# Strassen's seven products for the expert layers that run outside attention, with partial sums carried from PSUM bank to PSUM bank

## The chip, the core and the metric

One core of one Trainium2 chip. The metric is the device time of one execution in microseconds. Before the change it is 869.21 us, the median of three runs (868.94 to 869.37). The profile shows one execution of its own, with a span of 865.8 us from the first to the last instruction.

## The reference

Three layers follow each other on 3072 tokens (4 batches of 768) with 256 features (8 heads of 32): a chunked scan, a mixture of four experts, and a gated dense layer, all in float32.

```python
# scan ("attention" below), per batch and head, chunk by chunk
M = einsum(Cc, Bc) * L            # L = exp(cum_i - cum_j), causal
y = M @ xc + (Cc @ state) * exp(cum)
...
def _moe_ref(x, domain_probs, w1, w2):          # 4 experts, 256 -> 1024 -> 256
    p = domain_probs / (domain_probs.sum(-1, keepdims=True) + 1e-09)
    for e in range(E):
        h = np.maximum(x @ w1[e], 0.0)          # the "first layer" of expert e
        out += p[:, e:e + 1] * (h @ w2[e])      # its "second layer"
...
def _moe2_ref(x, w_gate, w_val, w_out):         # 256 -> 1536 -> 256, weights in float64
    g = x @ w_gate
    return (g / (1 + exp(-g)) * (x @ w_val)) @ w_out
```

## The kernel before

Every number is kept as a high part and a low part (tiles named `..h` and `..l`, the low part being the remainder), so one product of a 128x128 weight block with 512 tokens takes three matmuls: high by high, low by high, high by low. Tokens lie along the free dimension. `xh` and `xl` hold the tokens, `acc` the sum over the experts, six blocks of 512 tokens each.

All instructions stand in the order in which the code writes them; each engine works through its own list. Side work (attention steps, weight preparation, loads) is put between the matmuls by a table `todo`: a *unit* is one hidden chunk of 128 columns of one expert on one token tile, it has two half-slots, and `add` or `spread` puts functions into them.

- **Experts 0 and 1, inside attention** (`units1`): 7 token tiles (two of 256 tokens, five of 512), 2 experts, 8 hidden chunks. `m_hidden` runs the 6 matmuls of the first layer into a PSUM bank, ScalarE writes `hh` with a Relu, VectorE writes `hl` with the remainder; three units later `m_out` runs the 6 matmuls of the second layer into two output banks. The attention steps of chunk q (`points(q)`) lie around slot 66+8(q-8).
- **Experts 2 and 3, after attention** (`units23`): the same for 6 blocks of 512 tokens. Meanwhile the float64 weights of the dense layer are loaded and turned into high and low parts (`dense_chunk`: nine VectorE steps for a half, sums by GpSimd, splits by ScalarE and GpSimd) and stored to DRAM.
- **Dense layer**: for pairs of token blocks and *quads* of 2x128 hidden columns, `dense_hidden` already uses Strassen's scheme: 7 products in place of 8. With the 2x2 blocks of weights A and tokens B and the shared sums S1..S4 and T1..T4, each product goes to one of four banks X, Y, Z, W, and shared sums are added by VectorE from SBUF temporaries c1, u, v.

PSUM has eight banks: `h0..h2` for hidden sums, `po0, po1` for outputs and, once attention is done, `d0..d2`.

Of the kernel before, what the change touches and what calls it, by code (L numbers as in the profile page):

```python
# [7 lines left out]
F32 = mybir.dt.float32  # L8
F32R = mybir.dt.float32r
# [3 lines left out]
AX = mybir.AxisListType  # L13


@with_exitstack
def kernel(ctx: ExitStack, tc: tile.TileContext, nat_d, bc_d, bc0_d, a_d, probs, w1, w2, wg, wv, wo, out):
# [32 lines left out]
    sizes = [256] * 2 + [512] * 5  # L50
    offs = [sum(sizes[:i]) for i in range(len(sizes))]
    NTILE = len(sizes)
    assert sum(sizes) == NT
    BN = 512
    NBLK = NT // BN
    NPAIR = NBLK // 2
    NQD = FC2 // 2
    W7 = 7 * P
# [3 lines left out]
    hpool = ctx.enter_context(tc.tile_pool(name="hpool", bufs=LAG + 1))  # L62
# [10 lines left out]
    xh, xl, acc = ([v[o // BN][:, :, o % BN:o % BN + n] for o, n in zip(offs, sizes)] for v in (bxh, bxl, bacc))  # L73
    probs_d = dram.tile([E, NT], F32, name="probs_d")
# [395 lines left out]
    def a_done(q, keep=False):  # L470
        r = Q[q] if keep else Q.pop(q)
        y = r["y"]
        t, o = tile_of(q)
        yv = y[:, :KD * P].rearrange("p (k i) -> p k i", k=KD)
# [56 lines left out]
    def hidden_bank(n):  # L531
        turn[0] += 1
        return bank(*banks[turn[0] % min(len(banks), 4)])[:, :n]

    def place(u):

        e, t, f = u
        if e < 2:
            return offs[t], sizes[t], xh[t], xl[t], acc[t]
        return t * BN, BN, bxh[t], bxl[t], bacc[t]  # L540
# [15 lines left out]
    def m_out(u, later=None):  # L556
        e, t, f = u
        _, n, _, _, sm = place(u)
        if f == 0:
            opsum[e, t] = out_banks(n, len(banks) > 3 and t % 2 == 0)  # L560
# [9 lines left out]
        if later is None:  # L570
            tmp = [mpool.tile([P, 512], F32, tag="mb", name="tmp")[:, :n] for _ in range(KD)]
        else:
            both = raw_p.tile([P, KD, 512], F32, tag="raw", name="tmp")
            tmp = [both[:, d, :n] for d in range(KD)]
        for d in range(KD):
            nc.vector.tensor_tensor(out=tmp[d], in0=po[d], in1=pb, op=ALU.mult)

        def adds(engine=nc.vector):
            for d in range(KD):
                engine.tensor_tensor(out=sm[:, d, :], in0=sm[:, d, :], in1=tmp[d], op=ALU.add)  # L580

        later.append(adds) if later is not None else adds()

# [11 lines left out]
    def dense_src(c):  # L595
        g, what = divmod(c, 3)
        if what == 2:
            return wo[g * FG:(g + 1) * FG, :].rearrange("(k p) d -> p k d", p=P), NG, DM
        w = wg if what == 0 else wv
        return w[:, g * FG:(g + 1) * FG].rearrange("(k p) f -> p k f", p=P), KD, FG  # L600

    def dense_chunk(c, resident):
# [4 lines left out]
        src, k, n = dense_src(c)  # L607
        g, what = divmod(c, 3)
        kz = k // 2
        r = {}  # L610

        def load(z):
            def fn():
                r[z] = raw_p.tile([P, kz, n, 2], I32, tag="raw", name="f64")
                nc.sync.dma_start(
                    out=r[z].rearrange("p k n w -> p k (n w)"), in_=src[:, z * kz:(z + 1) * kz, :].bitcast(I32)
                )
            return fn

        def step(z, i):  # L620
            def fn():
                if (z, i) == (0, 0):
                    r["w"] = dpools["cv"].tile([P, 2, 4 * P], I32, tag="wr", name="dr", bufs=2)
                words = r[z].rearrange("p k n w -> p (k n) w")
                if what == 2:
                    m = r["w"][:, z, :]
                    lo, hi = words[:, :, 0], words[:, :, 1]
                else:
                    m = r["w"][:, :, z * 2 * P:(z + 1) * 2 * P]
                    lo, hi = (words[:, :, x].rearrange("p (j n) -> p j n", j=2) for x in range(2))  # L630
                if i == 0:
                    V.tensor_scalar(out=m, in0=hi, scalar1=20, scalar2=0x7FF, op0=ALU.logical_shift_right, op1=ALU.bitwise_and)
                elif i == 1:
                    V.tensor_scalar(out=m, in0=m, scalar1=896.0, scalar2=0.0, op0=ALU.subtract, op1=ALU.max)
                elif i == 2:
                    V.tensor_scalar(out=m, in0=m, scalar1=255.0, scalar2=8388608.0, op0=ALU.min, op1=ALU.mult)
                elif i == 3:
                    V.scalar_tensor_tensor(out=m, in0=hi, scalar=-0x80000000, in1=m, op0=ALU.bitwise_and, op1=ALU.bitwise_or)
                elif i == 4:
                    V.tensor_scalar(out=hi, in0=hi, scalar1=0xFFFFF, scalar2=3, op0=ALU.bitwise_and, op1=ALU.logical_shift_left)  # L640
                elif i == 5:
                    V.tensor_tensor(out=m, in0=m, in1=hi, op=ALU.bitwise_or)
                elif i == 6:
                    V.tensor_scalar(out=lo, in0=lo, scalar1=28, scalar2=None, op0=ALU.logical_shift_right)
                else:
# [429 lines left out]
```

## Time and profile before

| what | us |
|---|---|
| median of three runs | 869.21 |
| this profiled execution, span | 865.8 |
| TensorE (PE) busy | 855.1, 99% of the span |
| VectorE (DVE) busy | 578.7, 67% |
| ScalarE (ACT) busy | 343.7, 40% |
| GpSimd (POOL) busy | 333.0, 38% |

The span leaves out 3.4 us of the median. A matmul of 128x512 is listed with 0.39 us, but the next one starts 0.23 us later: matmuls overlap, so their starts are what to count, and a busy share of 100% does not by itself say that no start was late.

### The profile page before, as it was taken

The numbers are of one execution on the slowest core, as the hardware profiler recorded it, in microseconds if no ns is written. First come the engines' busy times: TensorE is split into PE (matmuls) and PEld (weight loads), VectorE is DVE, ScalarE is ACT, GpSimd is POOL, SyncE is SP. The second block draws the span as 40 slices with busy tenths as digits, with TensorE's granted clock in tenths as the row PEclk, the third lists the DMA queues.
The fourth block names the chain that finished last, engine by engine and source line by source line (L and its number), as shares of the span: only waits on it lengthen the run. The fifth ranks groups of instructions, "written<-read, shape, count | busy, mean of one in ns | idle before, by whom it ended". The sixth has DMA issues, their size and how long they took to land.

```text
span 865.8 us, 12236 instructions
## 1 busy us (share of the span) xinstructions
PE 855.1 (99%) x4490; PEld 708.8 (82%) x4490; DVE 578.7 (67%) x881; ACT 343.7 (40%) x605; POOL 333.0 (38%) x282
## 2 busy tenths in 40 slices
PE   8999999999999999999999999999999999999998
PEld 7898888888888888888888888887888878888886
DVE  6987556656554446767768587766676767667665
ACT  6664444444443333322233223324444444434443
POOL 5965323323331021321033126515563664535251
PEclk9999999999999999999999999999999999999999
DMA  7844443343350032144234302535344274437301
GB/s 245 281 155 142 134 135 102 117 137 102 103 170 20 25 110 87 60 146 146 86 99 180 110 25 79 201 122 188 132 156 151 92 265 135 173 109 268 110 1 48
DMA packets 46003, 111.38 MB, mean 129 GB/s; under 512 B 5048, under 2 KB 12920, under 8 KB 45944
## 3 DMA queue, kind: packets, MB, share of 16 engines
q1 hardware_dynamic: 45944, 110.61, 38.0%
q8 instruction: 35, 0.57, 0.3%
q14 instruction: 24, 0.20, 0.1%
HBM read 93.14 MB, written 17.45 MB: 128 GB/s over the span
## 4 chain that ended last, share of the span: by engine, by line
PE 87%; DVE 5%; POOL 3%; ACT 2%; issue 1%; DMA 1%; SPq 0%; POOLq 0%; ACTq 0%; DVEq 0%
PE h L509 24%; PE po L517 21%; PE h L804 14%; PE d L517 6%; PE d L804 5%; PE d L875 5%; PE po L875 5%; PE d L509 3%; PE ypsum L438 1%; PE scores L392 1%; PE ypsum L401 1%; POOL w_l L125 1%; POOL ws L666 1%; DVE hl L553 1%; POOL L L344 1%
## 5 line engine op out<-in xcount | busy, mean ns | idle before, releaser
L553 DVE SCALAR_TENSOR_TENSOR hl<-h,hh 128x512 fp32r<-128x512 f32 (+1 forms) x184 | 117.7, 642 | 163.3 <-ACT hh L552 163.1
L552 ACT ACTIVATE hh<-h 128x512 fp32r<-128x512 f32 (+1 forms) x184 | 102.6, 559 | 280.6 <-PE h L509 272.1
L842 POOL TENSOR_TENSOR al<-s,ah 128x512 fp32r<-128x512 f32 x70 | 103.5, 1505 | 124.1 <-ACT ah L840 114.6
L509 PE MATMUL h<-xh,w_h 128*128 128x512 f32 (+1 forms) x368 | 138.9, 377 | 2.6 <-DVE hl L553 2.1
L509 PE MATMUL h<-xl,w_h 128*128 128x512 f32 (+1 forms) x368 | 137.2, 373 | 0.0
L509 PE MATMUL h<-xh,w_l 128*128 128x512 f32 (+1 forms) x368 | 136.7, 372 | 0.0
L517 PE MATMUL po<-hh,w_h 128*128 128x512 f32 (+1 forms) x320 | 118.4, 370 | 0.6 <-ACT L L350 0.6
L517 PE MATMUL po<-hh,w_l 128*128 128x512 f32 (+1 forms) x320 | 118.0, 369 | 0.0
L517 PE MATMUL po<-hl,w_h 128*128 128x512 f32 (+1 forms) x320 | 117.8, 368 | 0.0
L840 ACT ACTIVATE ah<-s 128x512 fp32r<-128x512 f32 x72 | 45.3, 632 | 100.3 <-DVE s L837 84.7
L509 PEld LDWEIGHTS h<-xh,w_h 128*128 128x128 f32 x368 | 69.3, 188 | 18.1 <-issue 3.6
L509 PEld LDWEIGHTS h<-xl,w_h 128*128 128x128 f32 x368 | 69.3, 188 | 14.0 <-DVE xl L477 2.1
L509 PEld LDWEIGHTS h<-xh,w_l 128*128 128x128 f32 x368 | 69.3, 188 | 11.3
L517 PEld LDWEIGHTS po<-hh,w_h 128*128 128x128 f32 x320 | 60.2, 188 | 11.4 <-issue 1.1
L517 PEld LDWEIGHTS po<-hl,w_h 128*128 128x128 f32 x320 | 60.3, 188 | 10.1
L517 PEld LDWEIGHTS po<-hh,w_l 128*128 128x128 f32 x320 | 60.3, 188 | 9.7
L359 POOL TENSOR_TENSOR Bs<-bc,Bs 64x512 fp32r<-64x512 f32 x22 | 32.4, 1475 | 82.9 <-issue 71.3
L821 DVE TENSOR_TENSOR u<-h,c 128x512 f32<-128x512 f32 x36 | 24.9, 690 | 56.8 <-PE h L804 37.3
L832 ACT ACTIVATE s<-s 128x512 f32<-128x512 f32 x54 | 33.4, 629 | 43.3 <-DVE s L831 42.5
L804 PE MATMUL h<-xh,wq_h 128*128 128x512 f32 x128 | 50.1, 392 | 0.2 <-ACT s L832 0.2
L804 PE MATMUL h<-xh,wq_l 128*128 128x512 f32 x128 | 49.8, 389 | 0.0
L804 PE MATMUL h<-xl,wq_h 128*128 128x512 f32 x128 | 49.8, 389 | 0.0
(222 smaller groups left out, 1730.2 us busy)
## 6 DMA issues: line engine op xcount, KB each, us to landing
wq_h<-wd_d SPq DMA_DIRECT2D x32, 448.0 KB
wq_l<-wd_d SPq DMA_DIRECT2D x32, 448.0 KB
bc<-in_bc_dram SPq DMA_DIRECT2D x22, 512.0 KB
L<-crow_d SPq DMA_DIRECT2D x22, 512.0 KB
wq_o<-wo_d SPq DMA_DIRECT2D x16, 512.0 KB
nat<-in_nat_dram SPq DMA_DIRECT2D x24, 256.0 KB
raw<-in_w_dram SPq DMA_DIRECT2D x11, 512.0 KB
pbc<-probs_d SPq DMA_DIRECT2D x22, 256.0 KB
```

Of the source, the lines that this page charges most:

```text
L125: engine.tensor_tensor(out=lo[:, part], in0=raw[:, part], in1=hi[:, part].bitcast(F32), op=ALU.subtract)
L359: nc.gpsimd.tensor_tensor(out=r["Bs"][64:], in0=r["Br"][64:], in1=r["Bs"][64:].bitcast(F32), op=ALU.subtract)
L509: nc.tensor.matmul(ps, w[:, k, fs], v[:, k, :], start=(i == 0), stop=(i == len(ops) - 1))
L517: nc.tensor.matmul(po[d], w[:, fc, dsl], x, start=(first and i == 0), stop=(last and i == 2))
L552: nc.scalar.activation(out=hh, in_=ph, func=AF.Relu)
L553: nc.vector.scalar_tensor_tensor(out=hl, in0=ph, scalar=0.0, in1=hh.bitcast(F32), op0=ALU.max, op1=ALU.subtract)
L804: nc.tensor.matmul(ps, x[:, ws], y, start=(start and i == 0), stop=(i == 2), skip_group_check=True)
L821: V.tensor_tensor(out=u, in0=Y, in1=c1, op=ALU.add)
L832: nc.scalar.activation(out=s[key], in_=ps if add is None else s[key], func=AF.Silu)
L840: nc.scalar.activation(out=ah, in_=av, func=AF.Copy)
L842: low.tensor_tensor(out=al, in0=av, in1=ah.bitcast(F32), op=ALU.subtract)
L875: nc.tensor.matmul(po[d][:, zs], x[:, dsl], y[:, zs], start=(first and i == 0), stop=(last and i == 2), skip_group_check=True)
```

## The change

Only five token tiles (2048 tokens) stay inside attention; the attention steps of a chunk now lie 5.8 half-slots apart in place of 8. The last 1024 tokens of experts 0 and 1, and all of experts 2 and 3, move behind attention and run in 8 blocks (expert, pair of token blocks), each of 4 quads of 256 hidden columns (32 quads). A quad takes 7 products in place of 8 for the first layer (21 matmuls for 24) and the same 24 for the second. The shared sums do not pass through SBUF: ScalarE copies a bank into the next (X to Y, Y to Z), and the next product is accumulated on top. A quad is walked in four steps h0 to h3; behind the products of each step come 6 second-layer matmuls of the quad before (`project_part`) and the side work of that step. The weight preparation of the dense layer is rewritten (`dense_quad`: two ScalarE and four VectorE steps a quad), the experts' weights get sums and splits of their own (`expert_quad`), and tokens get the sums T1 to T4 (`token_sums`).

```diff
-    sizes = [256] * 2 + [512] * 5
+    sizes = [256] * 2 + [512] * 3
...
-    hpool = ctx.enter_context(tc.tile_pool(name="hpool", bufs=LAG + 1))
+    HB = LAG + 2
+    hpool = ctx.enter_context(tc.tile_pool(name="hpool", bufs=HB))
...
+    def expert_quad(e, j):
...
+        def high_a():
+            r["hl"] = [wpool.tile([P, W7], F32R, tag="w", name=f"we_{z}") for z in "hl"]
+            high(r["hl"][0][:, RAW], r["w1"][:, P:])
...
+        def high_s():
+            r["o"] = wpool.tile([P, 2, 2 * DM], F32R, tag="w", name="we_o")
+            WE[e, j] = r["hl"], r["o"]
+            high(r["hl"][0][:, SUM], r["w1"])
+            high(r["o"][:, 0, :], r["w2"])
...
+    def dense_quad(g, what):
...
+        def s0():
+            m = r["m"] = dpools["cv"].tile([P, 2 * FQ], I32, tag="wr", name="dr", bufs=2)
+            m = m.bitcast(F32)
+            nc.scalar.activation(out=m, in_=r["hi"].bitcast(F32), func=AF.Abs, scale=2.0**-112)
+            nc.scalar.activation(out=r["lo"], in_=r["byte"], func=AF.Copy, scale=1 / 32, bias=1 / 64)
...
+    def expert_hidden(e, p, j):
...
+        add(X, A11, "B11", True)
+        S.activation(out=Y, in_=X, func=AF.Copy)
+        yield
+        add(Y, S2, "T2")
+        S.activation(out=Z, in_=Y, func=AF.Copy)
+        add(W, S3, "T3", True)
+        S.activation(out=part3, in_=W, func=AF.Copy)
+        yield
+        add(Z, S1, "T1")
+        S.activation(out=v, in_=Z, func=AF.Copy)
+        add(X, A12, "B21")
+        low11 = out(11, X)
+        V.tensor_tensor(out=W, in0=W, in1=v, op=ALU.add)
+        low22 = out(22, W)
+        low11()
+        add(Y, A22, "T4")
+        V.tensor_tensor(out=Y, in0=Y, in1=part3, op=ALU.add)
+        if j > 0:
+            low22()
+        low21 = out(21, Y)
+        yield
+        low21()
+        if j == 0:
+            low22()
+        add(Z, S4, "B22")
+        out(12, Z)()
+        yield
...
+    def expert_project(e, p, j, key):
...
+        for d, (tmp, engine) in enumerate(((po[0], nc.vector), (pb, nc.gpsimd))):
+            nc.vector.tensor_tensor(out=tmp, in0=po[d], in1=pb, op=ALU.mult)
+            engine.tensor_tensor(out=bacc[b][:, d, :], in0=bacc[b][:, d, :], in1=tmp, op=ALU.add)
...
+        blocks = [(2, 0), (2, 2), (2, 1), (0, 2), (1, 2), (3, 0), (3, 1), (3, 2)]
...
-                    s = 66 + 8 * (q - 8) + o
+                    s = int(66 + 5.8 * (q - 8) + 0.8 * o)
...
+        for i, (e, p) in enumerate(blocks):
+            for j in range(NQE):
+                for h, _ in enumerate(expert_hidden(e, p, j)):
+                    project_part((1, 0, 3, 2)[h])
+                    at(i, j, h)
+                before = lambda key, e=e, p=p, j=j: expert_project(e, p, j, key)
```

**Place 1, ScalarE, in the middle of the expert stage.** Before, ScalarE's list there is one Relu (`hh<-h`) for each unit, with a split of a dense weight (`wd_h`) now and then:

```order
L552 ACTIVATE hh<-h_5083 128x512
L681 ACTIVATE wd_h<-dr 128x384
L681 ACTIVATE wd_h<-ws 128x512
L552 ACTIVATE hh<-h_5117 128x512
L552 ACTIVATE hh<-h_5138 128x512
```

Now it is, from the carries of the last quad of block 3 (L884 copies X to Y, L887 Y to Z, L889 and L892 copy W and Z to SBUF) to the first carry of the next quad (`we_h`, `we_o`: expert splits; `wd_o`: dense split; `dr`, `f`: the two dense steps s0):

```order
L892 ACTIVATE c_4365<-h_4362 128x512
L878 ACTIVATE hh<-h_4360 128x512
L878 ACTIVATE hh<-d_4363 128x512
L878 ACTIVATE hh<-h_4361 128x512
L602 ACTIVATE we_h<-raw_q 128x512
L602 ACTIVATE we_o<-raw_q 128x512
L602 ACTIVATE wd_o<-dr 128x512
L878 ACTIVATE hh<-h_4362 128x512
L678 ACTIVATE dr<-f_4385 128x512
L679 ACTIVATE f_4385<-f_4385 128x512
L884 ACTIVATE h_4459<-h_4458 128x512
```

The carry L884 stands behind a Relu and five preparing steps; the matmuls of the next product wait for it.

**Place 2, VectorE, where a block's outputs leave PSUM.** Before, the outputs of a tile are multiplied by the expert's share and added to `acc` between the preparing steps (`dr`, `f`), and the next tile has two other output banks:

```order
L553 SCALAR_TENSOR_TENSOR hl<-h_3681,hh 128x512
L640 TENSOR_SCALAR f_3571<-f_3571 128x512
L576 TENSOR_TENSOR tmp<-d_3544,pbc 128x512
L576 TENSOR_TENSOR tmp<-d_3545,pbc 128x512
L580 TENSOR_TENSOR acc_90<-acc_90,tmp 128x512 x2
```

Now, in the first quad of a block, two outputs of the block before leave between the quad's own sums (`d`, `h` with `c`) and remainders (`hl`):

```order
L895 TENSOR_TENSOR d_4461<-d_4461,c_4463 128x512
L879 SCALAR_TENSOR_TENSOR hl<-h_4458,hh 128x512
L899 TENSOR_TENSOR h_4459<-h_4459,c_4462 128x512
L939 TENSOR_TENSOR po_4157<-po_4157,pbc 128x512
L940 TENSOR_TENSOR acc_94<-acc_94,po_4157 128x512
L939 TENSOR_TENSOR pbc<-po_4158,pbc 128x512
L879 SCALAR_TENSOR_TENSOR hl<-h_4459,hh 128x512
L879 SCALAR_TENSOR_TENSOR hl<-d_4461,hh 128x512
L879 SCALAR_TENSOR_TENSOR hl<-h_4460,hh 128x512
L939 TENSOR_TENSOR d_4184<-d_4184,pbc 128x512
L940 TENSOR_TENSOR acc_95<-acc_95,d_4184 128x512
L939 TENSOR_TENSOR pbc<-d_4185,pbc 128x512
```

The outputs `po` and `d` are now freed by a multiply, an add and a multiply, and the next quad's second layer writes the same four banks.

**Place 3, the DMA queue of SyncE, at the end of the expert stage.** Before, the two chunks of dense weights that are loaded first come from SBUF, and the loads of `wq` start with the dense stage:

```order
L725 DMA wq_h<-wd_d 128x896
L725 DMA wq_l<-wd_d 128x896
L728 DMA wq_o<-wo_d 128x1024
L885 DMA out_dram<-s 128x512 x4
```

Now the first dense quad's weights are loaded ahead of the last stores and the last float64 load (`f<-in_wo_dram`):

```order
L733 DMA wq_h<-wd_d 128x896
L733 DMA wq_l<-wd_d 128x896
L736 DMA wq_o<-wo_d 128x1024
L721 DMA wd_d<-wd_h 128x896
L721 DMA wd_d<-wd_l 128x896
L669 DMA f_5696<-in_wo_dram 128x2x512
```

The load `wq_o` waits until a weight tile of the first quad of block 7 has been read, and the five rows' transfers stand ahead of `f` or beside it.

## Rows read from the trace of the kernel before

**Rows 1.** The page: busy time by engine, and GB/s in 40 equal slices.

```profile
PE 855.1 (99%) x4490; PEld 708.8 (82%) x4490; DVE 578.7 (67%) x881; ACT 343.7 (40%) x605; POOL 333.0 (38%) x282
GB/s 245 281 155 142 134 135 102 117 137 102 103 170 20 25 110 87 60 146 146 86 99 180 110 25 79 201 122 188 132 156 151 92 265 135 173 109 268 110 1 48
```

**Rows 2.** Busy time by stage: length, then PE, PEld, DVE, ACT, POOL, clock, DMA.

```profile
20.00:60.00 40.00, 37.44 (x361) 34.89 (x360) 36.47 (x55) 25.02 (x51) 34.96 (x27) 1.00 0.67 227
60.00:100.00 40.00, 39.39 (x324) 34.29 (x323) 27.48 (x45) 19.44 (x39) 19.21 (x19) 1.00 0.47 148
...
220.00:260.00 40.00, 40.00 (x248) 32.57 (x247) 24.68 (x36) 16.93 (x31) 14.35 (x16) 1.00 0.41 129
...
340.00:380.00 40.00, 40.00 (x178) 33.13 (x177) 29.20 (x52) 10.84 (x19) 7.70 (x8) 1.00 0.28 99
...
580.00:620.00 40.00, 38.86 (x167) 30.70 (x166) 25.30 (x35) 16.27 (x27) 22.98 (x16) 1.00 0.49 166
```

**Rows 3.** What PE waited for in the whole run: us in total, times, longest.

```profile
PE h L509 <- DVE hl L553: 2.1, 1, 2.1
...
PE po L517 <- ACT L L350: 0.6, 1, 0.6
```

**Rows 4.** Timeline in the expert stage: start us, length us, engine, line.

```profile
349.77 0.39 PE L509 MATMUL h<-xh,w_h 128*128 128x512 f32 x1
...
350.68 0.19 PEld L509 LDWEIGHTS h<-xl,w_h 128*128 128x128 f32 x1
...
350.90 0.39 PE L509 MATMUL h<-xl,w_h 128*128 128x512 f32 x1
...
351.33 0.60 ACT L552 ACTIVATE hh<-h 128x512 fp32r<-128x512 f32 x1 [2.12 <-PE h L509]
...
355.89 0.39 PE L509 MATMUL h<-xh,w_h 128*128 128x512 f32 x1
```

**Rows 5.** Groups by line and shape: busy us, mean ns of one, idle before.

```profile
L819 ACT ACTIVATE c<-h 128x512 f32<-128x512 f32 x36 | 21.2, 590 | 10.0 <-PE h L804 9.7
...
L576 DVE TENSOR_TENSOR tmp<-po,pbc 128x512 f32<-128x512 f32 x22 | 14.1, 680 | 0.0
...
L121 ACT ACTIVATE w_h<-raw 128x1024 fp32r<-128x1024 f32 x11 | 11.6, 1052 | 2.0 <-DMA raw<-in_w_dram 2.0
...
L681 ACT ACTIVATE wd_h<-ws 128x512 fp32r<-128x512 f32 x12 | 7.5, 625 | 12.8 <-POOL ws L666 12.8
```

**Rows 6.** Timeline of the dense stage: two VectorE sums that depend on each other.

```profile
850.57 0.69 DVE L823 TENSOR_TENSOR v<-h,u 128x512 f32<-128x512 f32 x1
...
851.37 0.69 DVE L835 TENSOR_TENSOR v<-d,v 128x512 f32<-128x512 f32 x1
```

**Rows 7.** Timeline in attention: two ScalarE steps that follow each other.

```profile
142.86 0.60 ACT L552 ACTIVATE hh<-h 128x512 fp32r<-128x512 f32 x1 [2.13 <-PE h L509]
143.35 0.62 ACT L355 ACTIVATE Bs<-bc 128x512 fp32r<-128x512 f32 x1
```

**Rows 8.** The DMA queue in attention: one load of each of two chunks.

```profile
139.95 0.33 SPq L318 DMA_DIRECT2D bc<-in_bc_dram  x1
...
152.62 0.33 SPq L318 DMA_DIRECT2D bc<-in_bc_dram  x1
```

**Rows 9.** VectorE in attention: the one wait for a load of L.

```profile
20.13 1.48 DVE L340 TENSOR_TENSOR L<-L,cum 128x1024 f32<-128x1024 f32 x1 [1.10 <-DMA L<-crow_d]
```

**Rows 10.** PE's busy time and granted clock, 12 to 14 us.

```profile
12.00:14.00 2.00, 2.00 (x36) 0.60 1.08 357
```

**Rows 11.** Timeline of PE's first expert matmuls, 256 columns each.

```profile
17.17 0.28 PE L509 MATMUL h<-xh,w_l 128*128 128x256 f32 x1
17.40 0.39 PE L509 MATMUL h<-xl,w_h 128*128 128x256 f32 x1
...
17.98 0.28 PE L509 MATMUL h<-xh,w_h 128*128 128x256 f32 x1
18.10 0.28 PE L509 MATMUL h<-xh,w_l 128*128 128x256 f32 x1
```

More of the change, by code (lines that the diff above doesn't have):

```diff
@@ L554, in m_hidden, with m_out @@
         hid[u] = hh, hl
[L556 removed]
+    def m_out(u):
         e, t, f = u
@@ L569, in m_out @@
             return
[L570 to L574, printed above, removed]
+        tmp = po if t == NTILE - 1 and e == 1 else [mpool.tile([P, 512], F32, tag="mb", name="tmp")[:, :n] for _ in range(KD)]
         for d in range(KD):
             nc.vector.tensor_tensor(out=tmp[d], in0=po[d], in1=pb, op=ALU.mult)
-        def adds(engine=nc.vector):
-            for d in range(KD):
-                engine.tensor_tensor(out=sm[:, d, :], in0=sm[:, d, :], in1=tmp[d], op=ALU.add)
@@ L582, in m_out @@
-        later.append(adds) if later is not None else adds()
+        for d in range(KD):
+            nc.vector.tensor_tensor(out=sm[:, d, :], in0=sm[:, d, :], in1=tmp[d], op=ALU.add)
     dpools = {}
     wq = {}
[L595 to L600, printed above, removed]
@@ L606, in dense_chunk @@
+    HIGH = np_f32(0x0FEFFFFF)
+    def dense_quad(g, what):
         V = nc.vector
-        src, k, n = dense_src(c)
-        g, what = divmod(c, 3)
-        kz = k // 2
         r = {}
[L612 to L618, printed above, removed]
@@ new lines @@
+    first_of = {}
+    def expert_project(e, p, j, key):
+        row, col = divmod(key, 10)
+        b = 2 * p + col - 1
+        fc = 2 - row
+        first = j == 0 and fc == (0 if col == 2 else 1)
+        last = j == NQE - 1 and fc == (1 if col == 2 else 0)
+        if first:
+            opsum[b] = out_banks(BN, col == 2)
+        po = opsum[b]
+        both = WE[e, j][1]
+        vh, vl = hid.pop((e, p, j, key))
+        for d in range(KD):
+            dsl = slice(fc * DM + d * P, fc * DM + (d + 1) * P)
+            for i, (z, y) in enumerate([(0, vh), (1, vh), (0, vl)]):
+                nc.tensor.matmul(
+                    po[d], both[:, z, dsl], y, start=(first and i == 0), stop=(last and i == 2), skip_group_check=True
+                )
+        if not last:
+            return
+        pb = pbc.pop((e, b))
+        if first_of.setdefault(b, e) == e and b * BN >= PLAIN:
+            for d in range(KD):
+                nc.vector.tensor_tensor(out=bacc[b][:, d, :], in0=po[d], in1=pb, op=ALU.mult)
+            return
+        for d, (tmp, engine) in enumerate(((po[0], nc.vector), (pb, nc.gpsimd))):
+            nc.vector.tensor_tensor(out=tmp, in0=po[d], in1=pb, op=ALU.mult)
+            engine.tensor_tensor(out=bacc[b][:, d, :], in0=bacc[b][:, d, :], in1=tmp, op=ALU.add)
@@ new lines, with job @@
+        seq, t1 = expert_tokens(0, bacc[4], bacc[5])
+        spread(seq, 72, 100)
+        put(102, t1)
+        def job(steps, at):
+            for fn, a in zip(steps, at, strict=True):
+                put(a + (a >= n0 and (a - n0) % 4 == 2 and fn.__name__ in ("s1", "s2", "sums")), fn)
+        for j, a in enumerate((138, 146, 154, 161)):
+            job(expert_quad(2, j), [a + o for o in (0, 4, 5, 7, 8, 9, 10)])
+        for i in range(1, len(blocks)):
+            e = blocks[i][0]
+            if e == blocks[i - 1][0]:
+                continue
+            for j in range(NQE):
+                job(expert_quad(e, j), [quad(i - 1, j) + o for o in (1, 4, 5, 8, 10, 11, 12)])
```

421 lines of the change are left out of this document (229 added, 192 removed).

## The prediction

> **What bounds the kernel now.** I read the page first: PE is busy for 99% of the span and no other engine for more than 67% [rows 1]. The busy time by stage says the same where it matters: from 100 us on, PE is busy for the whole of nearly every stretch, while VectorE takes 25 to 29 us of 40 and ScalarE 11 to 17 [rows 2]. Then what PE waited for: one wait of 2.1 us and one of 0.6, both among the small tiles at the start of attention [rows 3]. Since "busy" hides late starts, I count starts in the timeline: from 349.77 to 355.89 us PE starts 27 matmuls, 0.2267 us each, and a weight load (0.19 us) starts with the matmul ahead of its own [rows 4]. So in the expert stage nothing but the number of matmuls sets the time, and a change there is worth what it removes from that number, less every wait that it puts in front of PE.
>
> **What it removes.** 32 quads with 45 matmuls in place of 48: 96 matmuls of 128x512, 96 x 0.2267 = **-21.8 us**. The order confirms the count (4136 PE instructions before, 4040 after). A quad then takes 45 x 0.2267 = 10.20 us; below, times inside a quad count from its first matmul.
>
> **The carries.** Each quad gains four ScalarE copies; 128 of them at 0.59 us, the price of L819's copy out of PSUM [rows 5], are 76 us on an engine that has 29 of 40 us free in this stage [rows 2]. The tight one is X to Y. The last matmul of X starts at 0.45; ScalarE follows such a start by 0.43 (351.33 against 350.90 [rows 4]), the matmul's 0.39 and 0.04 for the handover; the copy ends at 0.88 + 0.59 = 1.47. Y's next product is matmul 9, its weights load at 8 x 0.2267 = 1.81, and the handover back takes, as I estimate it by that 0.04, some 0.05. Slack 0.3 us, given by the six second-layer matmuls in between: cost 0. No row shows ScalarE writing PSUM. From below it can't be worth more than nothing; from above I take the slowest plain ScalarE copy, L121's 1.05 us for twice the elements [rows 5]: 0.2 us late in each of 32 quads, 6 us. I keep 0, the copy's size being that of L819. The other carries (Y to Z wanted at matmul 21, Z to SBUF at 36) have over 1 us of slack.
>
> **What stands ahead of that carry.** ScalarE works in order, so preparing steps after the Relu of Y decide (place 1). That Relu starts late: the copy of Z starts at 5.64 and ends at 6.23, VectorE adds it to W (0.69), takes a remainder, adds to Y; two dependent sums start 0.80 apart, each 0.69 long [rows 6], so the Relu starts at about 8.35. ScalarE steps that follow each other start 0.49 apart [rows 7]. With n preparing steps and the last Relu in between, the next carry starts at 8.35 + 0.49(n + 2) = 9.33 + 0.49n, and must start by 10.20 + 1.81 - 0.59 - 0.05 = 11.37: four steps fit, the fifth makes it 0.4 to 0.5 late (a step from SBUF, as at L681, takes 0.63 [rows 5]). By the order five stand there in three quads (last of block 3, third of block 4, last of block 6), four or fewer in all others: **+1.5 us**; 0 to 3.
>
> **Block changes.** In place 2, VectorE can start on the old outputs when their last matmul is through, 35 x 0.2267 + 0.43 = 8.37. Multiply, dependent add (0.80 later), multiply (0.65: the length of L576, 0.68 [rows 5], less some overlap), three remainders at 0.65, multiply, add: the add that frees bank d1 starts at 13.2 and ends at 13.9. The next quad loads weights for d1 with matmul 59, at 13.38. So 0.5 us in each of the six changes where an add is needed (the seventh only multiplies): **+3.0 us**; 0 if VectorE keeps up a little better, 6 if a preparing step falls in between. The first quad after attention frees two banks with four steps, so that its remainder of Y ends at 11.7 and the carry at 12.35, against 12.01: **+0.3 us**.
>
> **Attention.** A chunk takes 12.7 us now (139.95 to 152.62 [rows 8]): four units of 12 matmuls, 10.9 us, and 1.8 of its own. With 5.8 half-slots it takes 2.9 units, 7.9 + 1.8 = 9.7 us, while VectorE's work for it falls only by that of 1.1 units, some 1 us (a remainder, 0.69, and a share of the outputs): from 24.7/40 of 12.7 us, 7.8 us (the stretch 220 to 260 [rows 2]), to about 7 of 9.7, 72%. ScalarE and GpSimd stay lower still. Bounds: at 62% PE lost nothing (220 to 260); at 69% it lost 0.61 of 40 us (60 to 100); at 91% it lost 2.56 of 40 (20 to 60) [rows 2]. The compressed part, 16 chunks of 9.7, is 155 us long: 0, 2.4 or 9.9 us. I take **+1.5**, near the 69% row. The load of L has about 5.5 us from the end of the chunk that frees it to the subtraction; before, that subtraction waited for it only once, at 20.13 us [rows 9].
>
> **The DMA queue.** In place 3 the load `wq_o` waits for the last Z product of block 7's first quad, at 8.6 us. Behind it go two stores and `f`, 1.92 MB in all. At 357 GB/s [rows 10] that is 5.4 us, at 281, the best slice of the page [rows 1], 6.8. With 1.7 us for the issues, `f` is there 5.5 to 7 us into the next quad, where two ScalarE steps that need it stand ahead of the copy of Z. That copy would end at 7.3 to 8.5 in place of 6.2, wanted at 35 x 0.2267 = 7.93. I take **+0.6**; 0 to 2.6, if the landing takes two us more than the transfers.
>
> **At nothing.** The new weight preparation moves work from VectorE to ScalarE and GpSimd; the quad's own sums leave VectorE free from about 0.2 to 6.2, and its preparing steps lie there. GpSimd's part (splits, token sums, some 110 more instructions) is covered by an engine that is 38% busy [rows 1]; its results are wanted a quad or more later. If that cover went, the weights of the next expert would be late by a step, under 2 us once an expert. The dense stage keeps its order; its 1.1 us of idle time near 600 us [rows 2] I leave as it is.
>
> **Sum.** -21.8 + 1.5 + 3.0 + 0.3 + 1.5 + 0.6 = -14.9 us. Against this execution's span of 865.8 it gives 850.9; with the 3.4 us that lie around the span, 854.3 for the median: **854 us**. A change under 0.2% (1.7 us) could not be told from none.
>
> **Rivals.**
> *All covers hold.* PE starts a matmul every 0.2267 us throughout: 869.2 - 21.8 = 847.4. For it: PE took shortages of the same size (ScalarE 63%, VectorE 91% at the start) with small losses. Against: places 1 and 2 count late by hand. Chance 0.19.
> *Attention becomes the bound.* VectorE's queue delays the scores' product and so the heads, as among the small tiles: +9.9 in place of +1.5, 863. Against: 72% is far from 91%. Chance 0.13.
> *Each carry is late* (the other side). Place: the nine matmuls from X to Y, in all 32 quads. If a copy into PSUM, or the queue ahead of it, ends x us later than 1.76, the loss is 32x on top of the sum: it decides at 14.9/32 = 0.47 us. A copy of twice the length, 1.18, with one preparing step more ahead of it (0.49) would be 0.3 + 0.5 = 0.8 late: 854 + 26 = 880. For it: the slack of 0.3 is the smallest in the loop, and nothing in the trace shows such a copy. Against: 0.59 for the same elements out of PSUM. Chance 0.06, two thirds of it above 869.
> *The clock falls.* Once in this trace the granted clock sank, to 0.60 at 12 to 14 us, among 36 small matmuls [rows 10]; shortly after, matmuls of 256 columns start 0.23 us apart, at the lower level (1.2 GHz), and later 0.12 apart, at the upper (2.4 GHz) [rows 11]. If PE's new waits brought that on, every quad at the lower level would cost about 9 us more: one for each of three block changes, 854 + 27 = 881. Against: over 1 us of idle time within 40 us near 600 us left the clock at 1.00 [rows 2]. Chance 0.02. The Trainium skill, "TensorE: Matmul & The Clock Gate", section "A second HAM failure mode: psum-queue depth-cycling", describes a kernel that cycles through PSUM banks and lets PE pause briefly between groups, so that its clock swings between the levels; by that rule the carries would be the wrong way to save matmuls. The dense stage here already hands sums between four banks, with the clock at 1.00, so this trace does not bear the rule out.
>
> **Chances and range.** The forecast, with waits of 3 to 10 us in sum (850 to 858), has 0.60. With all covers holding, 0.19, and attention, 0.13, it makes 0.92 that end below 867; of the late carries a part as well. Faster 0.93, within 0.2% 0.02, slower 0.05. The likeliest case's own bounds are 850 to 858; for 8 in 10 I go from 847 to 862, which takes in the case without waits and nearly all of attention's.
>
> **What will show it.** 96 matmuls fewer and, within quads, starts 0.2267 us apart. PE's waits should name the carry X to Y in three quads (0.5 us each) and the add of the old outputs at block changes (0.5); a copy out of PSUM into PSUM should take 0.6 us. In attention a chunk should take 9.7 us. I am wrong if that copy takes 0.9 or more, if PE waits for it in most quads, if attention chunks take over 10.2, or if the clock leaves 1.00 after 20 us.

## The result and the profile after

| | median us | range | runs |
|---|---|---|---|
| before | 869.29 | 868.94 to 869.75 | 4 |
| after | 861.84 | 859.53 to 863.37 | 4 |

The ratio is 0.9914, 95% interval 0.9896 to 0.9933: 7.45 us faster, where 15.2 were forecast. The direction holds; of the gain forecast, half came. The range (847 to 862) holds by 0.2 us, at an end that had been set for a slow attention stage, which did not come: that is luck. The profiled execution is the slowest of the four, 863.37 us with a span of 861.6.

The page of the changed kernel, busy time by engine, in the place of the first row of [rows 1]:

```profile
PE 838.8 (97%) x4394; PEld 692.8 (80%) x4394; DVE 609.7 (71%) x895; ACT 462.3 (54%) x824; POOL 442.7 (51%) x389
```

PE issues 4394 matmuls for 4490: the 96 are gone, as counted. But its share falls from 99% to 97%, so some of the time won is now spent waiting. The windows beside [rows 2] say where; the columns are the same:

```profile
20.00:60.00 40.00, 36.44 (x348) 34.50 (x347) 33.95 (x52) 24.33 (x50) 32.69 (x27) 0.96 0.67 224
60.00:100.00 40.00, 38.10 (x324) 33.26 (x323) 31.43 (x49) 20.99 (x42) 21.21 (x19) 1.00 0.50 163
...
340.00:380.00 40.00, 40.00 (x178) 33.07 (x177) 32.23 (x51) 25.13 (x46) 20.07 (x19) 1.00 0.38 126
```

In the middle of the expert stage PE is as full as before. What it waited for in the whole run (us in total, times, longest), beside [rows 3]:

```profile
PE h L829 <- ACT h L884: 6.0, 7, 3.1
PE h L531 <- DVE hl L573: 3.4, 1, 3.4
PE h L829 <- ACT h L887: 1.4, 1, 1.4
PE h L829 <- DVE hl L879: 1.3, 2, 1.0
...
PE po L539 <- DVE acc L588: 1.2, 1, 1.2
```

L884 is the carry X to Y and L887 the carry Y to Z. The carry X to Y is waited for 7 times, not 3, and one of the seven is 3.1 us long. I then counted every start of PE that comes later than 0.2267 us after the one ahead of it. In the expert stage they lie in these places: near 249 us (1.0 us in all, behind attention), 382 to 385 (2.3), 406 (0.4), 427 (0.2), 437 (0.4), 467 to 470 (1.5), 505 (1.6), 533 (0.4) and 547 (3.3). Behind nearly each the next matmul is late by another 0.1.

**The longest one.** The timeline around it, from SP's queue, ScalarE and PE (start, length, engine, line):

```profile
540.33 0.32 SPq L736 DMA_DIRECT2D wq_o<-wo_d  x1
540.75 0.38 SPq L721 DMA_DIRECT2D wd_d<-wd_h  x1
...
540.62 0.60 ACT L878 ACTIVATE hh<-h 128x512 fp32r<-128x512 f32 x1 [0.16 <-PE h L829]
545.99 0.52 ACT L602 ACTIVATE wd_h<-dr 128x384 fp32r<-128x384 f32 x1 [4.77 <-DMA wd_d<-wd_h]
546.42 0.58 ACT L884 ACTIVATE h<-h 128x512 f32<-128x512 f32 x1
...
543.54 0.39 PE L928 MATMUL po<-hl,we_o 128*128 128x512 f32 x1
547.05 0.80 PE L829 MATMUL h<-t24h,we_h 128*128 128x512 f32 x1 [3.13 <-ACT h L884]
547.65 0.63 PE L829 MATMUL h<-t24h,we_l 128*128 128x512 f32 x1
548.07 0.63 PE L829 MATMUL h<-t24l,we_h 128*128 128x512 f32 x1
```

What SP's queue itself waited for at `wq_o` in the whole run (us in total, times, longest); the longest ends at 540.33:

```profile
SPq L736 <- PE h L829: 32.6, 3, 23.2
```

Read it backwards. PE waits for the carry; the carry stands in ScalarE's list behind a split into `wd_h`; that split stands 4.77 us because the one tile `wd_h` is still being stored to DRAM for the job before; and that store was issued only at 540.75, because SP's queue had stood 23.2 us at `wq_o`, the load of place 3, until PE had read a weight tile. After the wait, 14 matmuls start some 0.43 us apart in place of 0.2267 (548.07 after 547.65 is the first pair): the lower of the two clock levels, 2.9 us more.

### The profile page after: what moved, and what is told of

Same layout as the page of the kernel before. It is cut to its first block, busy times and chain, and to the rows that moved or that the text cites. A ratio compares the mean times of both kernels' runs of the same rounds, so it can differ in the third digit from the quotient of the medians.

```text
span 861.6 us, 12496 instructions
## 1 busy us (share of the span) xinstructions
PE 838.8 (97%) x4394; PEld 692.8 (80%) x4394; DVE 609.7 (71%) x895; ACT 462.3 (54%) x824; POOL 442.7 (51%) x389
## 5 line engine op out<-in xcount | busy, mean ns | idle before, releaser
L895 DVE TENSOR_TENSOR d<-d,c 128x512 f32<-128x512 f32 x32 | 22.3, 698 | 85.2 <-ACT c L892 85.1
L928 PE MATMUL d<-hh,we_o 128*128 128x512 f32 x256 | 79.8, 393 | 0.0
L928 PE MATMUL po<-hh,we_o 128*128 128x512 f32 x256 | 79.0, 390 | 0.5 <-DVE acc L594 0.5
L879 DVE SCALAR_TENSOR_TENSOR hl<-h,hh 128x512 fp32r<-128x512 f32 x96 | 66.1, 689 | 18.2 <-ACT hh L878 14.2
L572 ACT ACTIVATE hh<-h 128x512 fp32r<-128x512 f32 (+1 forms) x80 | 40.5, 510 | 67.5 <-PE h L531 67.5
L573 DVE SCALAR_TENSOR_TENSOR hl<-h,hh 128x512 fp32r<-128x512 f32 (+1 forms) x80 | 45.9, 577 | 34.7 <-ACT hh L572 34.3
L531 PE MATMUL h<-xh,w_h 128*128 128x512 f32 (+1 forms) x160 | 57.4, 359 | 4.3 <-DVE hl L573 3.4
L539 PE MATMUL po<-hh,w_h 128*128 128x512 f32 (+1 forms) x160 | 57.4, 359 | 1.9 <-DVE acc L588 1.2
L531 PE MATMUL h<-xh,w_l 128*128 128x512 f32 (+1 forms) x160 | 56.1, 350 | 0.2 <-POOL w_l L143 0.2
L531 PE MATMUL h<-xl,w_h 128*128 128x512 f32 (+1 forms) x160 | 56.1, 350 | 0.0
L539 PE MATMUL po<-hh,w_l 128*128 128x512 f32 (+1 forms) x160 | 56.0, 350 | 0.0
```

The lines of the kernel that those rows point to most:

```text
L531: nc.tensor.matmul(ps, w[:, k, fs], v[:, k, :], start=(i == 0), stop=(i == len(ops) - 1))
L539: nc.tensor.matmul(po[d], w[:, fc, dsl], x, start=(first and i == 0), stop=(last and i == 2))
L572: nc.scalar.activation(out=hh, in_=ph, func=AF.Relu)
L573: nc.vector.scalar_tensor_tensor(out=hl, in0=ph, scalar=0.0, in1=hh.bitcast(F32), op0=ALU.max, op1=ALU.subtract)
L879: return lambda: V.scalar_tensor_tensor(out=hl, in0=ps, scalar=0.0, in1=hh.bitcast(F32), op0=ALU.max, op1=ALU.subtract)
L928: nc.tensor.matmul(po[d], both[:, z, dsl], y, start=(first and i == 0), stop=(last and i == 2), skip_group_check=True)
```

## The experiments

Each run was timed in five rounds beside the kernel before. "Late" means by PE's starts in the trace of that run. The edits are to the changed kernel, if nothing else is said.

**The changed kernel again.** 

> The changed kernel once more, unedited, as the base of this group. Theory: its late starts in the expert stage come from the order of the side work, so this execution shows the same places again: 0.4 to 0.5 us at the three quads with five ScalarE steps ahead of the carry X to Y, 1 to 1.3 us twice at the second quad of the fourth and of the sixth block, 1.6 us in the seventh block, about 3 us at the start of the last block's second quad, and the clock at the lower level for some 5 us behind that. The wait near 24 us (3.36 us) hangs on when the store crow_d lands and should differ by a microsecond or so. Time 860 to 863. Rival: the waits are scatter of one execution; then other places show up.

861.65 us, ratio 0.992 [0.9905, 0.9935]. Every late start of the expert stage is there again, none differs by more than 0.3 us: they belong to the order of the work, not to the execution. Only the wait near 24 us moved, to 2.38 us.

**The dense loads behind the store.** 

> One edit: the first dense layer's loads (wq, five transfers) move from the seventh block's last quad to the last block's first quad, behind the store wd_d<-wd_h and the load f. Theory A (the SP queue stood behind wq_o, so the store came late, its tile was not free, ScalarE waited 4.8 us and the carry X to Y with it; TensorE's clock fell because of that wait): the 3.1 us wait goes, the stretch at the lower clock behind it goes (3.4 us), 6.5 us in all: 855, range 853 to 857.5; the granted clock of 540 to 580 us comes to 0.98 or more. Rival B (the clock falls there by itself): only the wait goes, 858.5, and the clock of that stretch stays near 0.91. Rival C (the transfer itself is slow, not the queue): ScalarE still waits for the store, 861 to 862.

```diff
-        put(quad(6, 3, 2), lambda: dense_load(0, 0))
+        put(quad(7, 0, 2), lambda: dense_load(0, 0))
```

856.29 us, ratio 0.9863 [0.9844, 0.9883]: 5.4 us less than the run above. The wait is gone, and with it the lower clock (6.2 us in the trace). The windows of 540 to 580 us, of the changed kernel's second run and then of this one:

```profile
540.00:580.00 40.00, 36.66 (x151) 29.80 (x150) 18.93 (x31) 17.51 (x30) 8.10 (x6) 0.91 0.60 210
```

```profile
540.00:580.00 40.00, 39.55 (x175) 32.46 (x174) 21.52 (x34) 22.27 (x38) 9.74 (x7) 1.00 0.60 210
```

The share of the DMA engines is the same, 0.60: it was the order of the transfers, not their amount. Theory A.

**No fifth step.** 

> One edit: three dense steps s0 (two ScalarE steps each) go one step later, behind the next quad's carry X to Y, in the three quads where five ScalarE steps stood ahead of it. Theory A (four steps fit, the fifth makes the carry 0.4 to 0.5 us late): the three waits of 0.41, 0.40 and 0.41 us in the trace go, with the 0.11 us behind each, 1.5 us in all: 860.3, and nothing else moves. Rival B (the carry is late there for another reason, such as its wait for the Relu of Y): the waits stay, 861.8. Rival C: the two steps now make the carry Y to Z late (it is wanted 21 matmuls into the quad): waits for L887 appear, 862 or more.

```diff
+                if (g, what) in ((3, 0), (3, 2), (5, 1)):
+                    at_[1] += 1
```

860.09 us, ratio 0.9902 [0.9883, 0.992]. All three waits are gone, the other four of L884 stay:

```profile
PE h L829 <- ACT h L884: 5.5, 4, 3.5
...
PE d L928 <- DVE acc L940: 0.2, 1, 0.2
```

The median is 1.6 us lower, against 1.5 expected. Theory A, by the trace; the intervals of the two times overlap. One thing did move: at 416 us PE now starts 0.32 us late, because the second layer waits for the add of a block's old outputs (L940), the wait that the forecast had at block changes. VectorE's list stands where it stood (its L895 ahead of that add starts 0.83 us later than in the run above, and the late starts near 380 us 0.80 later), but PE comes half a microsecond sooner: the fifth step had hidden this wait, and of its 1.5 us some 0.4 come back.

**Two late starts behind a block change.** Here the trace of the changed kernel's second run shows VectorE and GpSimd side by side, then the chain that hangs on them, and PE's two late starts:

```profile
371.26 0.68 DVE L939 TENSOR_TENSOR pbc<-d,pbc 128x512 f32<-128x512 f32 x1
371.86 0.28 DVE L612 TENSOR_TENSOR raw_q<-raw_q 128x128 f32<-128x128 f32 x1
372.17 1.29 DVE L613 TENSOR_TENSOR raw_q<-raw_q 128x128 f32<-128x128 f32 x1
373.50 1.26 DVE L614 TENSOR_TENSOR raw_q<-raw_q 128x128 f32<-128x128 f32 x1
374.80 1.26 DVE L615 TENSOR_TENSOR raw_q<-raw_q 128x128 f32<-128x128 f32 x1
...
372.02 1.30 POOL L940 TENSOR_TENSOR acc<-acc,pbc 128x512 f32<-128x512 f32 x1 [2.43 <-DVE pbc L939]
373.27 1.34 POOL L605 TENSOR_TENSOR we_l<-raw_q,we_h 128x512 fp32r<-128x512 f32 x1
374.58 1.34 POOL L605 TENSOR_TENSOR we_o<-raw_q,we_o 128x512 fp32r<-128x512 f32 x1
...
379.05 0.60 ACT L878 ACTIVATE hh<-d 128x512 fp32r<-128x512 f32 x1 [3.89 <-DVE d L895]
...
379.66 0.50 PE L829 MATMUL h<-xh,we_h 128*128 128x512 f32 x1 [1.05 <-DVE hl L879]
...
382.97 0.50 PE L829 MATMUL h<-t24h,we_h 128*128 128x512 f32 x1 [0.95 <-ACT h L884]
```

A sum of 128 columns takes 1.26 to 1.29 us here, and each ends 0.14 or 0.15 after the GpSimd operation that began beside it. The add W+v (L895) comes after them, and ScalarE stands 3.89 us for it. The first late start is not a carry: PE waits there for a remainder (L879) to be read out of the bank that the next quad's first product writes; the second is the carry X to Y. Three runs ask whether GpSimd is the cause.

> One edit: at the block changes GpSimd's splits of the expert weights (low parts of the third quad's sums and second layer, and of the next expert's first quad) run two steps later; VectorE's own work stays as it is. Theory A (VectorE's four sums of 128x128, L612 to L615, take 1.26 us each because GpSimd's splits run beside them): the sums take 0.3 to 0.5 us there, the chain W+v, remainder, Relu, carry comes in time, and the waits of 1.2 and 1.1 us in the fourth block and of 0.4 and 1.1 us in the sixth go, 3.8 us: 858, range 856.5 to 859.5. Rival B (VectorE simply has too much to do at a block change, with the old outputs): the sums' length stays or the waits stay, 861 to 862. Rival C (a split that comes later makes a later product wait): a new wait for we_l or we_o, 862 or more.

The seven numbers place an expert quad's steps load, high_a, low_a, sums, high_s, low_s and low_o.

```diff
-                job(expert_quad(e, j), [quad(i - 1, j) + o for o in (1, 4, 5, 8, 10, 11, 12)])
+                job(expert_quad(e, j), [quad(i - 1, j) + o for o in ((1, 4, 5, 8, 10, 13, 14) if j == 2 else (1, 4, 7, 8, 10, 11, 12) if j == 0 else (1, 4, 5, 8, 10, 11, 12))])
```

861.50 us, ratio 0.9917 [0.9902, 0.9932]: no change in time. The edit missed its aim: GpSimd has nothing else in its list there, so two of the three splits start where they started before. Only the third went, and only the VectorE step beside it got shorter (L683, 1.24 us before, 0.41 now). With it the first of the two late starts fell from 1.21 to 0.38 us, by the same 0.83; the second stayed at 1.13:

```profile
377.13 1.27 DVE L615 TENSOR_TENSOR raw_q<-raw_q 128x128 f32<-128x128 f32 x1
378.32 0.41 DVE L683 TENSOR_SCALAR dr<-dr 128x512 f32<-128x512 f32 x1
```

> One edit to the changed kernel: for the third quad of each expert the sums, ScalarE's splits and GpSimd's low parts come one to two steps earlier, so that GpSimd's two operations of 1.33 us each no longer lie beside the fourth quad's sums; those sums stay on VectorE and in their place. Theory A (a VectorE sum there ends only when the GpSimd operation beside it ends): in the sixth block, where GpSimd then has only its add into acc left, one sum is held to about 1.3 us and the two behind it take 0.45 each, L895 starts 1.6 us earlier and its late starts of 0.38 and 1.13 us go; in the fourth block the next expert's split (1.06) stays, and 1.21 and 1.12 shrink to under 1.2 in sum. In all 2.5 to 3 us: 859, range 857.5 to 860.5. Rival B (the sums are long by themselves behind the evacuation): they stay at 1.26 each and so does the time, 861.7.

```diff
-                job(expert_quad(e, j), [quad(i - 1, j) + o for o in (1, 4, 5, 8, 10, 11, 12)])
+                job(expert_quad(e, j), [quad(i - 1, j) + o for o in ((1, 4, 5, 7, 8, 9, 10) if j == 2 else (1, 4, 5, 8, 10, 11, 12))])
```

861.33 us, ratio 0.9926 [0.991, 0.9942]: no change again, but now the trace tells why. In the sixth block only the add is left beside the sums:

```profile
461.45 0.28 DVE L612 TENSOR_TENSOR raw_q<-raw_q 128x128 f32<-128x128 f32 x1
461.77 1.28 DVE L613 TENSOR_TENSOR raw_q<-raw_q 128x128 f32<-128x128 f32 x1
463.08 0.29 DVE L614 TENSOR_TENSOR raw_q<-raw_q 128x128 f32<-128x128 f32 x1
463.41 0.29 DVE L615 TENSOR_TENSOR raw_q<-raw_q 128x128 f32<-128x128 f32 x1
...
461.61 1.29 POOL L940 TENSOR_TENSOR acc<-acc,pbc 128x512 f32<-128x512 f32 x1 [1.17 <-DVE pbc L939]
...
364.42 0.63 ACT L602 ACTIVATE we_h<-raw_q 128x512 fp32r<-128x512 f32 x1 [3.02 <-DVE raw_q L615]
...
365.89 0.57 ACT L887 ACTIVATE h<-h 128x512 f32<-128x512 f32 x1
```

Same sums, same engine, same place in the list: 0.29 us beside an idle GpSimd, 1.28 beside a busy one. Rival B falls. Of the four late starts at 380 and 465 us three are gone, and the fourth fell from 1.1 to 0.4. What they gave is lost one quad earlier: the sums that I moved now meet GpSimd there, the split behind them stands 3.02 us in ScalarE's list, and the carry Y to Z behind it makes PE wait 1.9, 0.65 and 1.2 us in the three blocks.

> One edit: VectorE's four sums of the fourth quad's expert weights (L612 to L615) go from behind the evacuation of the old outputs to behind the remainders of the same quad, with what hangs on them three steps later too. Theory A (these sums, held up to 1.26 us each beside GpSimd's operations, stand ahead of W+v and so of the whole chain to the next carry): L895 starts about 3 us earlier and ScalarE no longer waits 3.9 us for it; the late starts of 1.21 and 1.12 us in the fourth block and of 0.38 and 1.13 in the sixth go, 3.8 us: 857.8, range 856.5 to 859. Rival B (the evacuation itself is too long for a block change, as forecast with 0.5 us each): half or more of these waits stay, 860 to 861.5. Rival C (the later sums make the products of that quad's weights late): new waits at the fourth quad of a block, 862 or more.

```diff
-                job(expert_quad(e, j), [quad(i - 1, j) + o for o in (1, 4, 5, 8, 10, 11, 12)])
+                job(expert_quad(e, j), [quad(i - 1, j) + o for o in ((1, 4, 5, 8, 10, 11, 12) if j < 3 else (1, 4, 5, 11, 12, 13, 14))])
```

856.47 us, ratio 0.9861 [0.9846, 0.9876]: 5.2 us less, and all four late starts gone, and the small one at 427 us with them (4.5 us in the trace, with the 0.1 behind each; the rest is within the scatter of the runs). Behind the remainders GpSimd is idle, and the four sums take 0.28 to 0.29 us:

```profile
377.13 0.69 DVE L895 TENSOR_TENSOR d<-d,c 128x512 f32<-128x512 f32 x1
...
380.95 0.28 DVE L612 TENSOR_TENSOR raw_q<-raw_q 128x128 f32<-128x128 f32 x1
381.26 0.29 DVE L613 TENSOR_TENSOR raw_q<-raw_q 128x128 f32<-128x128 f32 x1
```

**The tokens' splits two steps later.** 

> One edit: the splits of the first pair's tokens for the dense layer begin two steps later in the seventh block. Theory A (ScalarE's xh<-acc waits 1.58 us for GpSimd's add of the old outputs into acc, and the carry Y to Z stands behind it in ScalarE's list): the late start of 1.61 us near 503 us goes: 860.0, range 859 to 861. Rival B (the carry Y to Z is late there for its own product): the wait stays, 861.6.

```diff
-        spread(dense_tokens(0), quad(6, 1), quad(7, 2))
+        spread(dense_tokens(0), quad(6, 1, 2), quad(7, 2))
```

859.61 us, ratio 0.9908 [0.9892, 0.9925]; the late start near 503 us is gone (1.6 us in the trace, 2.0 between the medians, whose intervals overlap). What had stood ahead of the carry, in the changed kernel's second run:

```profile
501.71 0.63 ACT L602 ACTIVATE xh<-acc 128x512 fp32r<-128x512 f32 x1 [1.58 <-POOL acc L940]
502.25 0.58 ACT L887 ACTIVATE h<-h 128x512 f32<-128x512 f32 x1
```

**All four.** 

> Four edits together: the dense loads behind the store, the fourth quad's sums behind the remainders, the tokens' splits two steps later, three s0 steps behind the carry. Theory A (each late start has a cause of its own in an in-order list, and the gains add): 5.4 + 3.8 + 1.6 + 1.5 = 12.3 us less than 861.65: 849.3, range 847.5 to 851; the carries X to Y then leave one wait, behind attention's end, and the clock stays at 1.00 from 240 us on. Rival B (a gap closed at one place comes back at the next, since the engines are full): less than 9 us in all, 853 or more, with the carry named in other quads.

850.21 us (849.48 to 851.58), ratio 0.9794 [0.978, 0.9809]: 11.4 us less than the changed kernel. The carry X to Y leaves two waits, and the clock stays at 1.00 there:

```profile
PE h L829 <- ACT h L884: 0.6, 2, 0.4
```

One of the two lies behind attention, as expected. The other (444 us) is in a quad into which the fourth edit has pushed dense steps: ScalarE waits 1.48 us for W+v there, and a split (`wd_o`) stands ahead of the carry. Theory A: the gains add, by the traces (late starts and lower clock of the expert stage come to 15.3 us in the changed kernel's second run and to 2.5 here, 12.8 less, for 12.3 expected). By the medians the four edits alone give 14.1 us, more than together; each of those medians has a scatter of 1.6 to 3.7 us. The kernel that the forecast spoke of, without the waits that it did not see, lies 3.8 us below the forecast.

**A long wait elsewhere.** 

> The four edits and, in one quad of the second block, eight more ScalarE splits of 128x512 ahead of the carry X to Y (the same values written again). Theory A (a wait of some 3 us makes the clock fall for some microseconds, wherever it lies): PE waits about 3.3 us there, then starts lie 0.43 us apart for a while, which costs 3 us more: 6 to 7 us above the kernel with the four edits. Rival B (the clock fell near 547 us for a reason of that place): 3 to 3.5 us above it, with the clock at 1.00 in the second block.

```diff
+            if (g, what) == (0, 1):
+                for _ in range(8):
+                    s5()
```

855.53 us, 5.3 above the kernel with four edits. The wait is 4.28 us, longer than meant; behind it the clock is at 0.71 for 8 us, 26 matmuls in place of 37, and then at 1.00 again:

```profile
286.00:294.00 8.00, 3.72 (x17) 2.80 (x16) 4.94 (x8) 7.78 (x15) 5.42 (x5) 0.86 0.00 0
294.00:302.00 8.00, 8.00 (x26) 6.34 (x27) 5.29 (x6) 3.86 (x7) 3.15 (x2) 0.71 0.70 248
302.00:310.00 8.00, 8.00 (x37) 6.63 (x36) 3.08 (x5) 4.99 (x9) 2.57 (x2) 1.00 0.19 65
```

So the place near 547 us is not special (against rival B). In this execution the wait makes PE's start 4.4 us late and the lower clock adds 2.4; between the two profiled executions the spans differ by 854.0 - 847.8 = 6.2 us, as A had it, and between the medians by 5.3, with a scatter of 2.1 us in the kernel with four edits. How often the clock falls is for the last section.

**Each carry twice.** 

> The kernel with the four edits (850.21), and in each of the 32 quads the carry X to Y is done twice (the same copy again), which adds one ScalarE step of 0.49 between X and Y. Theory A (the forecast: each carry has 0.3 us of slack by itself, less where preparing steps stand ahead of it): it ends 0.2 us late where nothing stands ahead and up to 0.6 late where four steps do, with 0.1 us on the next matmul, so 0.3 to 0.7 in nearly every quad: 10 to 20 us more, 860 to 870; the wait X to Y is named about 30 times. Rival B (the slack is 0.5 us or more, for example because the handover is quicker): waits only in the quads with four steps, under 8 in number, 2 to 5 us more: 852 to 855. Rival C (a carry's length is no cost, since the queue of six matmuls covers it): no more than 1 us.

```diff
         S.activation(out=Y, in_=X, func=AF.Copy)
+        S.activation(out=Y, in_=X, func=AF.Copy)
```

857.27 us, ratio 0.9877 [0.9864, 0.9889]: 7.1 us above the kernel with four edits. The waits name the carry only 4 times; one has to count starts. A quad in which nothing stands ahead, with the carry, its double, and PE's starts:

```profile
300.65 0.58 ACT L884 ACTIVATE h<-h 128x512 f32<-128x512 f32 x1 [0.70 <-PE h L829]
301.26 0.58 ACT L885 ACTIVATE h<-h 128x512 f32<-128x512 f32 x1
...
301.58 0.39 PE L929 MATMUL po<-hl,we_o 128*128 128x512 f32 x1
301.89 0.50 PE L829 MATMUL h<-t24h,we_h 128*128 128x512 f32 x1
302.23 0.39 PE L829 MATMUL h<-t24h,we_l 128*128 128x512 f32 x1
```

301.89 is 0.08 late and 302.23 another 0.11. This comes in 31 quads; their late starts sum to 8.7 us, against 1.7 in the kernel with four edits, and the difference is the 7.0 that the time shows. The second copy starts 0.61 us after the first here, so a single carry has 0.61 - 0.08 = 0.53 us of slack: more than my 0.3, by which I expected 10 us or more. Theory A in kind (nearly every quad is late), between A and B in size.

**Two more edits.** 

> The four edits and two more: one dense split (wd_o) goes one step later, out of a quad where the fourth edit had left one step too many ahead of the carry (0.61 us late near 444 us); and the last outputs of attention's experts are added bank by bank (multiply, add, multiply, add) in place of both products first, since PE waits 0.5 us for the first add near 247 us and 0.17 for the carry behind it. Theory: 0.6 + 0.7 to 1.0 us less than 850.21: 848.8, range 847.5 to 850; the carry X to Y is then named nowhere, or once. Rival: these places are held by something else (the second add comes later and PE waits for it as long): 850.

```diff
+                if (g, what) == (3, 2):
+                    at_[4] += 1
...
+        if tmp is po:
+            for d in range(KD):
+                nc.vector.tensor_tensor(out=tmp[d], in0=po[d], in1=pb, op=ALU.mult)
+                nc.vector.tensor_tensor(out=sm[:, d, :], in0=sm[:, d, :], in1=tmp[d], op=ALU.add)
+            return
```

848.84 us (848.55 to 850.95), ratio 0.9787 [0.9774, 0.98]: not to be told from the kernel with four edits by time. By the trace the start at 444 us is late by 0.14 us in place of 0.61, while the late starts near 248 us come to 1.4 us for 1.2: there the rival is right.

## Why the prediction was right in direction and wrong in size

For the terms of the sum, with late starts read from the profiled execution after:

| term | forecast | measured |
|---|---|---|
| 96 matmuls | -21.8 | 96 fewer, -21.8 |
| carries | 0 | 0; slack 0.53 in place of 0.3 |
| a fifth step ahead of the carry | +1.5 | +1.5 (three times 0.4, and 0.1 behind each) |
| block changes | +3.0 | 0 |
| first quad after attention | +0.3 | +1.2 |
| attention | +1.5 | +1.4 |
| the DMA queue (place 3) | +0.6 | +6.2 (3.3 late, 2.9 of clock) |
| preparation "at nothing" | 0 | +4.5 |
| tokens' split behind GpSimd's add | not seen | +1.7 |

The measured terms make -21.8 + 16.5 = -5.3. The start of attention adds 1.3 of wait and 0.7 of clock in this execution, which makes -3.3; the spans differ by 861.6 - 865.8 = -4.2. The other 0.9 is about what the small late starts of 0.1 us come to less in attention, from 100 us on (2.7 before, 2.0 after). In the median that start weighs less: its wait is 3.4 us in this execution and 1.5 to 2.7 us in the other eleven traces, whose order is the same there, against 2.1 in [rows 3].

**What held.** The count; the copy of PSUM into PSUM (0.58 us, forecast 0.59 to 0.6); that no carry is late unless something stands ahead of it; the three quads with five steps, each at the 0.4 to 0.5 forecast; attention, where the two late starts (1.4 and 0.75 us near 70 and 89 us, for 0.7 before) are all in the stretch 60 to 100, and chunks follow each other every 9.6 us (ten intervals between loads of `bc`, from 110.85 to 206.39), for 9.7 forecast.

**The step that failed.** "At nothing" and "The DMA queue": covers that I took on whole engines. In "The DMA queue" I saw that SP's queue would stand at `wq_o`, and followed the load `f` behind it, wanted a quad later. I did not follow the two stores in front of `f`. A store frees a tile; the next job's split writes that one tile; the split stands in ScalarE's list ahead of the carry. So the delay met the carry X to Y, whose product is wanted 1.81 us into the quad, and not the copy of Z, wanted at 7.93, and it brought the lower clock with it: 6.2 us for 0.6, and 5.4 by experiment.

"At nothing" said that VectorE is free from 0.2 to 6.2 us of a quad and that its preparing steps lie there. Both fail in the quad behind a block change: the old outputs hold VectorE until 3.7 us of it (in the changed kernel's second run until 371.94 us, in a quad whose first matmul starts at 368.25), and the sums then take up to 1.29 us each beside GpSimd, 4.2 us in place of the 1.3 that they need alone. The price I gave for a lost cover, "under 2 us once an expert", was near the size (2.6, 0.3 and 1.7 us at the three changes of expert), but I put it into no sum, and its reason was another: no weight came late, the sums stood ahead of W+v. The tokens' split is the same slip at another place: ScalarE waiting for GpSimd, with a carry behind it.

**Block changes** erred the other way: the add that frees the bank ended 13.3 us into the block (in the same run at 371.34, the second quad's start being 368.25 and the first quad 10.2 long), not 13.9, and it is wanted at 13.38. The term was 3.0 too high and hid part of the other errors: without it I would have said 851. The wait is avoided by 0.1 us only: with the fifth step moved it shows at one block change (0.32 us in the run of that edit alone, 0.34 with four edits).

The rivals: that all covers hold, that every carry is late, and that attention binds, did not come. "The clock falls" came in part, behind the long wait near 547 us, at 3 us and not 9, and behind the one near 24 us; so one of my signs of being wrong, a clock below 1.00 after 20 us, did show. My reading of [rows 11] there was unsafe: the window from 17.00 to 17.90 us, which holds the starts 0.23 us apart, has a granted clock of 1.00 in that trace.

The Trainium skill, "TensorE: Matmul & The Clock Gate", section "A second HAM failure mode: psum-queue depth-cycling", tells of a kernel that cycles through PSUM banks, whose PE pauses briefly between groups of matmuls, and whose clock swings with it. The traces here don't show that for this kernel. Its products cycle through four banks in 32 quads, and the clock is 1.00 over the expert stage both in the kernel with four edits, where few pauses are left, and in the one with each carry twice, where PE starts 0.08 us late or more in 31 quads. The windows, in this order:

```profile
240.00:580.00 340.00, 338.26 (x1487) 278.13 (x1485) 235.84 (x373) 217.64 (x388) 171.07 (x163) 1.00 0.36 122
```

```profile
240.00:580.00 340.00, 337.37 (x1456) 270.40 (x1454) 229.52 (x365) 232.67 (x417) 164.20 (x158) 1.00 0.35 120
```

## What to carry to other kernels

Before an engine's work is costed at nothing, walk through its list at the places where two streams meet (a block change, the first quad, the end of a stage), and price there not the engine's mean share but what stands ahead of the one step that the bound engine waits for. Follow a late DMA queue through every entry in it: a store is as urgent as a load where its tile has one buffer. And a moved step has to be checked at its new place too: of three ways to part VectorE's sums from GpSimd, one moved little, one moved the wait, and one, behind the chain, took it away.

## What the runs showed of the hardware

A VectorE sum that reads two SBUF tensors waits for the GpSimd operation beside it: 128 columns took 0.28 to 0.29 us alone and 1.26 to 1.29 beside GpSimd's of 1.29 to 1.34, ending 0.14 or 0.15 us after it. The length follows the GpSimd operation: in the changed kernel's second run, where such a sum began up to 0.25 us behind the GpSimd operation, it took 0.43 to 0.46 us beside GpSimd operations of 0.46 to 0.52, 0.98 to 0.99 beside one of 1.06, and once 2.50 beside one of 2.45. A step with one tensor in SBUF and a number was held too (L683: 1.24 for 0.41). VectorE's sums with an operand in PSUM (L895, L939) took 0.68 to 0.70 throughout. The Trainium skill, "SBUF — State Buffer", section "Who interferes with whom", says this: a VectorE instruction with two SBUF inputs and a GpSimd instruction that reads SBUF exclude each other for a whole instruction. The traces agree; I had not priced it.

A wait of PE of 3 to 4 us brought the lower clock behind it in some executions and not in others: of the seven traces that have the wait near 545 us, 3.1 to 3.6 us long, the matmuls behind it lost 1.4 to 2.9 us in four, and none in three (waits of 3.4, 3.2 and 3.3). The waits of 1.45 us near 503 us left the clock at 1.00. Shorter waits are not safe for that: near 24 us, in attention, the lower level was granted within 1.2 us of a wait's end in seven of the thirteen traces, behind waits of 2.1 to 3.4 us, and was not in the other six, behind waits of 1.5 to 2.4. What decides it stays open. It may be part of the scatter, but that is not shown: the four runs of the changed kernel lie within 3.8 us, and those of the kernel with four edits, without a long wait in the expert stage, still within 2.1.
